# Regrouped deviations in a Fourier filter with a SoLU layer: laid out by a small matrix product in place of a store and a reload

## Chip, core and metric

The kernel runs on one core of one Trainium2 chip. The metric is the device time of one execution in microseconds (us). The core has TensorE (PE, matrix products; its weight loads are shown apart as PEld), VectorE (DVE), ScalarE (ACT), GpSimd (POOL) and SyncE (SP). Each engine works through its own instructions in order. DMAs are issued from SP, ACT and POOL, as instructions in these engines' order: an issue that has to wait holds up what stands behind it on that engine.

## What is computed

```python
def _attn_ref(x, filt_r, filt_i):                 # x: (8, 3136, 256) fp32
    X = np.fft.rfft(x, axis=1)
    Y = X * (filt_r + 1j * filt_i)[None, :, :]
    return np.fft.irfft(Y, n=x.shape[1], axis=1).astype(np.float32)

def _moe_ref(x, w_in, w_out, g_ln):               # x: (25088, 256), w_in: (256, 1024), w_out: (1024, 256)
    h = x @ w_in
    e = np.exp(h - np.max(h, axis=-1, keepdims=True))
    solu = h * (e / (np.sum(e, axis=-1, keepdims=True) + 1e-09))
    mu = np.mean(solu, axis=-1, keepdims=True)
    var = np.mean((solu - mu) ** 2, axis=-1, keepdims=True)
    return (((solu - mu) / np.sqrt(var + 1e-06) * g_ln) @ w_out).astype(np.float32)

def reference(x, filt_r, filt_i, moe_w_in, moe_w_out, moe_g_ln):
    return _moe_ref(_attn_ref(x, filt_r, filt_i).reshape(8 * 3136, 256), moe_w_in, moe_w_out, moe_g_ln)
```

All is in fp32. The part that matters here is the factor 1/sqrt(var + 1e-06), one number for each of the 25088 tokens, by which a row of the output is scaled.

## The kernel before

**Two kinds of work in one loop.** The eight images go through a Fourier transform of 49 x 64 points, a filter and the transform back; the tokens that come out go through the layer with w_in and w_out. Image 0 is transformed ahead of the loop, image 1 in its first steps, and images 2 to 7 beside the layer's work on the tokens that are already there. A list, PLAN (lines 37 to 46), says in which step each piece of an image's transform runs; lists of jobs for each step (line 875) hold them. The order of all engines' instructions is the order in which `step(k)` (line 948) writes them down; nothing reorders it.

**Blocks, pairs and groups.** A block is 128 tokens; there are 196. Two blocks are a pair (98), two pairs a group (49 groups of 512 tokens). A pair takes two steps, an even and an odd one. Products over a pair are made by a scheme with seven products in place of eight (m = 1 to 7), with sums of operands made by POOL (`pair_sums`, `project_sums`). `product(j, m)` (line 715) is one of seven products of pair j with w_in, into the banks of `ps_m`; `project(p, m)` (line 834) is one of seven with w_out, four matmuls each, into two banks of `ps_o`: products 1, 5, 6 and 3 add up in bank 0 (tag o0), products 2, 7 and 4 use bank 1 (tag o1). A step k with j = k // 2 has products of pair j, and projections of pair j - 5 (even step: 5, 3, 4) or j - 4 (odd step: 1, 2, 6, 7).

**From h to the output.** For a block, ACT and DVE make h, e, and solu (lines 729 to 780); ACT's `square` (line 775) leaves the sum of squared differences in one column of a tile of 128 x 4 for the group. DVE's `turn` (line 782) transposes solu in squares of 32 x 32, and `regroup` (line 790) copies the result by eight DMAs of 128 KB per pair (solu_t<-turn), issued from SP, so that 1024 features stand in the partitions. By this the tokens are regrouped: a block of the second product holds 32 tokens of each of the four blocks of a group. `keep_out` (ACT, line 854) and `finish_out` (DVE, line 858) scale the projections by the deviations while they move them from PSUM into the output tile `ot`, and `store_out` (line 863) stores it with two DMAs from SP.

**The deviations.** The four columns of a group, one per block, stand in the old order of tokens, and are needed in the new one: number (32 a + r, b) has to come to (32 b + r, a), with a and b from 0 to 3 and r from 0 to 31. `deviations` (line 802) makes 1/sqrt(var/1024 + 1e-6) in `rs` by two POOL instructions, and stores the 2 KB in DRAM (`rows`); `regroup_deviations` (line 812) loads them back by four DMAs of 512 bytes, 32 partitions each, into `rs_t`. For the groups up to 47 these DMAs are issued from SP: the store in the even step of an odd j, behind the eight solu_t DMAs of that step and ahead of its two stores of the output; the four loads in the odd step that follows. For the last group they are issued from POOL. The first reader of `rs_t` is `keep_out(p, 0, (0, 0))` in the odd step of the pair after (line 1033).

**Rows and fetches.** For images 2 to 7, `fetch_quarters` (line 235) loads rows of x by SP; DVE's `difference` and POOL's `sum` (line 257, instruction at line 260) prepare them, PE's `first_quarters` (line 263, matmuls at line 269, tile pa) makes the first half of the transform, ACT moves it to SBUF (line 274), and POOL issues the store into DRAM (d1, line 280). `fetch` (line 288, DMA at line 291, tile t) loads it back, ordered by frequency; it waits for those stores. For images 2 to 7 the fetch is issued from ACT (line 913), in the middle of an even step, behind the move of product 3 of the projection. The first fetch of image 2 (e == 2, i == 0) alone is issued at the end of step 14. `fetch_de` loads a table, from ACT as well. `back_halves` (line 361) makes the last part of the transform back.

Of the kernel before, what the change touches and what calls it, by code (L numbers as in the profile page):

```python
# [9 lines left out]
FP32 = mybir.dt.float32  # L10
# [7 lines left out]
P = 128  # L18
# [76 lines left out]
def kernel(  # L95
# [16 lines left out]
    de_dram = nc.inline_tensor(de_host, name="de_tbl").ap()  # L112

    def pool(name, bufs, space=None, stack=ctx):
        kw = {} if space is None else {"space": space}
        return stack.enter_context(tc.tile_pool(name=name, bufs=bufs, **kw))
# [508 lines left out]
    rs_dram = pool("rs_dram", 2, DRAM)  # L625
    pools |= {name: pool(name + "1", bufs)
             for name, bufs in (("r", 4), ("diff", 1), ("t2", 1), ("p", 1), ("g", 1))}
    pools["de"] = pool("de1", 2)
    second.pools = pools
# [50 lines left out]
    def load_de(sp, u):  # L680
# [6 lines left out]
    turns, variances, solu_ts, solu_sums, rs_rows, rss, pos, ots = (  # L687
        {} for _ in range(8))
# [113 lines left out]
    def deviations(p, dma):  # L802
        g, second = divmod(p, 2)
        if not second:
            rs = small.tile([P, 4], FP32, name=f"rs_{g}", tag="rs", bufs=2)
            nc.gpsimd.tensor_scalar(out=rs, in0=variances.pop(g), scalar1=1.0 / DFF, scalar2=EPS_LN,
                                    op0=ALU.mult, op1=ALU.add)
            nc.gpsimd.tensor_tensor(out=rs, in0=rs, in1=neg_half, op=ALU.pow)
            rs_rows[g] = rows = rs_dram.tile([P, 4], FP32, name=f"rows_{g}", tag="rows")
            dma(out=rows, in_=rs)  # L810

    def regroup_deviations(g, dma):
        rows = rs_rows.pop(g).rearrange("(a p) b -> b p a", p=32)
        rss[g] = small.tile([P, 4], FP32, name=f"rs_t_{g}", tag="rs_t")
        for b in range(4):
            dma(out=rss[g][32 * b:32 * b + 32, :], in_=rows[b])
# [17 lines left out]
    def project(p, m):  # L834

        bank = {1: 0, 6: 0, 5: 0, 3: 0, 2: 1, 7: 1, 4: 1}[m]
        if m in (1, 2):
            pos[p, bank] = ps_o.tile([P, DFF // 2], FP32, name=f"o{m}_{p}", tag=f"o{bank}")[:, 0:P]
        s1, s2, s3, s4 = solu_sums[p]
        lhs = {1: solu_ts[p, 0][0], 2: solu_ts[p, 0][1], 4: solu_ts[p, 1][1], 5: s1, 6: s2, 7: s3,  # L840
               3: s4}[m]
        w = w_out_sb[:, {1: 0, 2: 1, 3: 2, 5: 3, 6: 4, 7: 5, 4: 6}[m]]
        for f in range(KF // 2):
            nc.tensor.matmul(out=pos[p, bank], lhsT=lhs[:, f, :], rhs=w[:, f, :],  # L844
                             start=f == 0 and m in (1, 2, 7), stop=True, skip_group_check=True)
# [37 lines left out]
    for e in range(1, B):  # L883
# [24 lines left out]
        for i, t in enumerate(spectrum_at):  # L908
# [4 lines left out]
            dma = nc.sync.dma_start if e == 1 and t < 8 else nc.scalar.dma_start  # L913
# [34 lines left out]
    def step(k):  # L948
# [23 lines left out]
        if not odd:  # L972
# [25 lines left out]
            if proj:  # L998
                project(p, 3)
                keep_out(p, 0, (0, 1))  # L1000
                project(p, 4)
            for job in spectrum_loads[k]:
                job()
# [3 lines left out]
            if j - 3 == pairs - 2:  # L1007
                deviations(j - 3, nc.gpsimd.dma_start)
            if 0 <= j - 4 < pairs:
                project_sums(j - 4, 1)  # L1010
            if j - 3 == pairs - 2:
                regroup_deviations((j - 3) // 2, nc.gpsimd.dma_start)
            elif 0 <= j - 3 < pairs:
                deviations(j - 3, nc.sync.dma_start)
# [9 lines left out]
        else:  # L1024
# [16 lines left out]
            if 0 <= j - 3 < pairs:  # L1041
                if (j - 3) % 2 == 0 and j - 3 < pairs - 2:
                    regroup_deviations((j - 3) // 2, nc.sync.dma_start)
# [24 lines left out]
    with tc.manual_schedule():  # L1068
        pair_sums(0)
        for load in first_loads:  # L1070
            load()
        for k in range(blocks + LAG):
            step(k)
# [30 lines left out]
```

## Time and profile before

Three runs took 1626.26 us in the median (1624.71 to 1630.68). The profiled execution took 1619.98 us.

| | us |
|---|---|
| median of three runs | 1626.26 |
| the profiled execution's own time | 1619.98 |
| its span, first to last instruction | 1618.2 |
| matmuls with w_out, o<-w_out_sb (L844), 5488 passes, busy | 402.1 and 311.0 |
| matmuls with w_in, m<-w_in_sb (L723), 1372 passes, busy | 396.6 and 308.0 |
| POOL rs, two instructions per group (L806, L808), mean ns of one | 275 and 1034 |
| DMAs rows<-rs from SP and POOL | 48 and 1 |
| DMAs rs_t<-rows from SP and POOL | 192 and 4 |

The mean granted TensorE clock is 0.991 of the full one. A profile page has one line for each group of instructions: the source line (L844), the engine, the operation, what it writes and reads (o<-w_out_sb,solu_t), the shape, the count, busy time and mean duration. In a timeline the first two numbers are start and duration in us; a bracket at the end tells how long the engine was idle before and what ended that. SPq and ACTq mark the issue of a DMA, not its transfer. Busy times of PE overlap, since one matmul begins before the last one has drained.

### The profile page before, as it was taken

To read this page: it belongs to the slowest core of one execution; us is meant where nothing else is said; L and a number is where in the kernel's file an instruction comes from. 1 tells how busy PE (TensorE), PEld (TensorE's weight loads), DVE (VectorE), ACT (ScalarE), POOL (GpSimd) and SP (SyncE) were. 2 spreads that over 40 slices of the span, in tenths; PEclk is the share of its full clock that TensorE was granted. 3 is DMA by queue.
4 is the path that set the end of the run, shared out by engine and by line. 5 is a ranking of instruction groups with operands and counts; after the bars stand their busy time and mean duration, and the time that the engine had idled before them with its cause. 6 is when DMAs were issued, how large, how long until landed. Compare 5 with 4: busy or idle time off the path is not lost. (4 is left out here: it accounts for less than half of the span.)

```text
span 1618.2 us, 37006 instructions
## 1 busy us (share of the span) xinstructions
PE 1548.8 (96%) x12710; PEld 1048.2 (65%) x12710; DVE 1302.4 (80%) x2630; ACT 903.4 (56%) x1772; POOL 1169.3 (72%) x1333
## 2 busy tenths in 40 slices
PE   5899899999999999999999999999999999999997
PEld 1363456666766677667766676667676777777776
DVE  1686877998898989997999789897988777777772
ACT  2135555566565655666656655566556566665662
POOL 4446887579777877797688867788666766677775
PEclk8999999999999999999999999999999999999999
DMA  9888878877788778866887668866785454444443
GB/s 268 245 268 249 244 208 229 223 209 196 203 246 231 201 189 243 241 192 167 211 251 200 186 180 229 238 180 169 215 234 151 121 135 122 104 112 105 110 110 102
DMA packets 377245, 312.13 MB, mean 193 GB/s; under 512 B 62762, under 2 KB 342835, under 8 KB 377059
## 3 DMA queue, kind: packets, MB, share of 16 engines
q1 hardware_dynamic: 304340, 168.63, 40.3%
q0 software_dynamic: 34624, 101.68, 20.7%
q10 hardware_dynamic: 38096, 39.46, 8.1%
q8 instruction: 103, 1.69, 0.5%
q14 instruction: 82, 0.67, 0.1%
HBM read 124.86 MB, written 81.50 MB: 128 GB/s over the span
## 5 line engine op out<-in xcount | busy, mean ns | idle before, releaser
L844 PEld LDWEIGHTS o<-w_out_sb,solu_t 128*128 128x128 f32 x3136 | 382.8, 192 | 49.3 <-issue 43.9
L723 PE MATMUL m<-w_in_sb,s 128*128 128x512 f32 x784 | 396.6, 607 | 9.9 <-ACT h L733 9.2
L844 PE MATMUL o<-w_out_sb,solu_t 128*128 128x128 f32 x3136 | 402.1, 276 | 2.9 <-DVE ot L860 2.0
L844 PEld LDWEIGHTS o<-w_out_sb,u 128*128 128x128 f32 x2352 | 307.3, 192 | 144.4 <-issue 109.7
L844 PE MATMUL o<-w_out_sb,u 128*128 128x128 f32 x2352 | 311.0, 275 | 7.4 <-ACT ot L856 4.6
L723 PE MATMUL m<-w_in_sb,y 128*128 128x512 f32 x588 | 308.0, 607 | 4.8 <-DVE h L744 2.9
L771 DVE SCALAR_TENSOR_TENSOR h<-e,rsum,h 128x1024 f32<-128x1024 f32 x196 | 302.1, 1541 | 6.9
L733 ACT COPY h<-m 128x512 f32<-128x512 f32 x294 | 172.9, 588 | 237.0 <-PE m L723 204.2
L702 POOL TENSOR_TENSOR u<-solu_t 128x512 f32<-128x512 f32 x98 | 133.3, 1361 | 219.3 <-DMA solu_t<-turn 134.6
L856 ACT ACTIVATE ot<-o,rs_t 128x128 f32<-128x128 f32 x392 | 143.6, 366 | 258.3 <-PE o L844 241.2
L779 ACT ACTIVATE h<-h,nmu 128x1024 f32<-128x1024 f32 x196 | 224.9, 1148 | 53.2 <-DVE turn L787 43.0
L747 DVE CUSTOM_DVE_ANT_0 h<-m,h 128x512 f32<-128x512 f32 x196 | 134.1, 684 | 140.3 <-ACT h L733 102.6
L787 DVE STREAM_TRANSPOSE turn<-h 128x1024 f32<-128x1024 f32 x196 | 243.2, 1241 | 3.2
L755 ACT ACTIVATE e<-h,nmax 128x1024 f32<-128x1024 f32 x196 | 225.1, 1149 | 8.8 <-DVE h L771 8.4
L702 POOL TENSOR_TENSOR u<-solu_t,u 128x512 f32<-128x512 f32 x98 | 149.0, 1520 | 93.4 <-PE o L844 89.2
L723 PEld LDWEIGHTS m<-w_in_sb,s 128*128 128x128 f32 x784 | 128.6, 191 | 98.3 <-issue 85.0
L860 DVE SCALAR_TENSOR_TENSOR ot<-o,rs_t,ot 128x128 f32<-128x128 f32 x294 | 102.0, 347 | 77.0 <-ACT ot L856 60.6
L723 PEld LDWEIGHTS m<-w_in_sb,y 128*128 128x128 f32 x588 | 96.3, 191 | 102.1 <-issue 52.9
L702 POOL TENSOR_TENSOR u<-u,solu_t 128x512 f32<-128x512 f32 x98 | 161.6, 1649 | 0.9
L702 POOL TENSOR_TENSOR solu_t<-solu_t,solu_t 128x512 f32<-128x512 f32 x98 | 153.4, 1565 | 7.7
L702 POOL TENSOR_TENSOR s<-y 128x128 f32<-128x128 f32 x196 | 95.6, 488 | 0.5
L372 PEld LDWEIGHTS py<-wb_t,t 50*64 50x64 f32 x3584 | 57.6, 134 | 42.9 <-issue 22.5
(116 smaller groups left out, 1965.4 us busy)
## 6 DMA issues: line engine op xcount, KB each, us to landing
solu_t<-turn SPq DMA_DIRECT2D x784, 128.0 KB
out_dram<-ot SPq DMA_DIRECT2D x196, 128.0 KB
t<-d POOLq DMA_DIRECT2D x112, 200.0 KB, 6.0
d<-x POOLq DMA_DIRECT2D x100, 200.0 KB, 5.1
f<-f_dram POOLq DMA_DIRECT2D x39, 512.0 KB, 7.2
d<-g POOLq DMA_DIRECT2D x39, 512.0 KB, 4.8
t<-d ACTq DMA_DIRECT2D x37, 512.0 KB
x<-in_x_dram SPq DMA_DIRECT2D x112, 98.0 KB
```

The lines of the kernel that those rows point to most:

```text
L372: nc.tensor.matmul(out=views[g][64 * h:64 * h + 64, cb, i, :], lhsT=t4[rows, i, c0:c0 + 64], rhs=wb_t[rows, 0:N1], start=True, stop=True)
L702: nc.gpsimd.tensor_tensor(out=out, in0=in0, in1=in1, op=op)
L723: nc.tensor.matmul(out=ms[j, bank], lhsT=lhsT, rhs=w_in_sb[:, w, :], start=m in (1, 2, 7), stop=True, skip_group_check=True)
L733: nc.scalar.copy(out=h_half(k, i), in_=ms[j, 0])
L747: nc.vector.tensor_tensor_reduce(out=h_half(k, i), in0=ms[j, bank], in1=h_half(*kept), scale=1.0, scalar=sofar, op0=ALU.add, op1=ALU.min, ...
L755: nc.scalar.activation(out=e, in_=hs[k], func=AFT.Exp, bias=nmaxs.pop(k)[:, 1:2], scale=-1.0, accum_out=esum)
L771: nc.vector.scalar_tensor_tensor(out=solu, in0=e, scalar=rsum, in1=solu, op0=ALU.mult, op1=ALU.mult, accum_out=nmu)
L779: nc.scalar.activation(out=solu, in_=solu, func=AFT.Square, bias=nmu, scale=-float(DFF), accum_out=variances[g][:, i:i + 1])
L787: nc.vector.transpose(out=turns[g][:, :, i, :], in_=solus[k].rearrange("p (f j) -> p f j", j=32))
L844: nc.tensor.matmul(out=pos[p, bank], lhsT=lhs[:, f, :], rhs=w[:, f, :], start=f == 0 and m in (1, 2, 7), stop=True, skip_group_check=True)
L856: nc.scalar.activation(out=out_half(p, *to)[0], in_=pos[p, 0], func=AFT.Copy, scale=rs)
L860: nc.vector.scalar_tensor_tensor(out=ot, in0=pos[p, bank], scalar=rs, in1=out_half(p, *kept)[0], op0=ALU.mult, op1=ALU.add)
```

## The change

The deviations no longer go through DRAM. A table `turn_t` of 128 x 36 is loaded once, by POOL: its first 32 columns hold a one where the partition's number modulo 32 equals the column's number, its last four a one where the partition divided by 32 does. `deviations(g)` makes `rs` as before and then, in a third POOL instruction, a tile `wide` of 128 x (4 x 32): element (p, b, i) is rs[p, b] where p modulo 32 is i, and zero elsewhere. `regroup_deviations(g, ps)` is a product on PE, with `wide` as the weights and the last four columns of the table as the moving side: it puts rs[32 a + r, b] at (32 b + r, a). Its result takes four columns of bank 1 of the projection, columns 128 to 131, behind the 128 that products 2, 7 and 4 use; ACT copies it from there to `rs_t`. The product stands in an even step of an even j, behind product 4 of the projection of pair j - 5, one pair before its result is read, and ahead of the fetches of that step; the first group, when there is no projection yet, uses a bank of `ps_t`. The last group goes the same way as the others. The five DMAs per group and the DRAM tile are gone.

Beside this the first fetch of image 2 is issued from SP, at the same place in the order of steps.

```diff
@@ -110,6 +110,10 @@
     wi_dram = nc.inline_tensor(wi_host, name="wi_tbl").ap()
     wb_dram = nc.inline_tensor(wb_host, name="wb_tbl").ap()
     de_dram = nc.inline_tensor(de_host, name="de_tbl").ap()
+    rows = np.arange(P)[:, None]
+    turn_dram = nc.inline_tensor(np.concatenate(
+        [rows % 32 == np.arange(32), rows // 32 == np.arange(4)], 1).astype(np.float32),
+        name="turn_tbl").ap()
 
     def pool(name, bufs, space=None, stack=ctx):
         kw = {} if space is None else {"space": space}
@@ -622,10 +626,11 @@
     hpool = pool("hp", 2)
     wk = pool("wk", 1)
     spool = pool("sp", 1)
-    rs_dram = pool("rs_dram", 2, DRAM)
     pools |= {name: pool(name + "1", bufs)
              for name, bufs in (("r", 4), ("diff", 1), ("t2", 1), ("p", 1), ("g", 1))}
     pools["de"] = pool("de1", 2)
+    spread = pool("spread", 1)
+    turn_t = spread.tile([P, 36], FP32, name="turn_t", tag="turn_t")
     second.pools = pools
     for c, at, n, kind, dims in (
             (0, 0, 4 * C, "t2", "p (v c) -> p v c"), (0, 4 * C, 4 * C, "f", "p (v k c) -> p v k c"),
@@ -684,8 +689,8 @@
                             in_=de_dram[i:i + pairs].rearrange("i p k u q -> p i (k u q)"))
         return de
 
-    turns, variances, solu_ts, solu_sums, rs_rows, rss, pos, ots = (
-        {} for _ in range(8))
+    turns, variances, solu_ts, solu_sums, spreads, rss, pos, ots, places = (
+        {} for _ in range(9))
     sums, ms, hs, nmaxs, es, solus, squares = {}, {}, {}, {}, {}, {}, {}
 
 
@@ -799,21 +804,22 @@
             nc.sync.dma_start(out=st[32 * q:32 * q + 32, :, :],
                               in_=turned[32 * a:32 * a + 32, :, q, :])
 
-    def deviations(p, dma):
-        g, second = divmod(p, 2)
-        if not second:
-            rs = small.tile([P, 4], FP32, name=f"rs_{g}", tag="rs", bufs=2)
-            nc.gpsimd.tensor_scalar(out=rs, in0=variances.pop(g), scalar1=1.0 / DFF, scalar2=EPS_LN,
-                                    op0=ALU.mult, op1=ALU.add)
-            nc.gpsimd.tensor_tensor(out=rs, in0=rs, in1=neg_half, op=ALU.pow)
-            rs_rows[g] = rows = rs_dram.tile([P, 4], FP32, name=f"rows_{g}", tag="rows")
-            dma(out=rows, in_=rs)
-
-    def regroup_deviations(g, dma):
-        rows = rs_rows.pop(g).rearrange("(a p) b -> b p a", p=32)
+    def deviations(g):
+        rs = small.tile([P, 4], FP32, name=f"rs_{g}", tag="rs", bufs=2)
+        nc.gpsimd.tensor_scalar(out=rs, in0=variances.pop(g), scalar1=1.0 / DFF, scalar2=EPS_LN,
+                                op0=ALU.mult, op1=ALU.add)
+        nc.gpsimd.tensor_tensor(out=rs, in0=rs, in1=neg_half, op=ALU.pow)
+        spreads[g] = wide = spread.tile([P, 4, 32], FP32, name=f"wide_{g}", tag="wide")
+        nc.gpsimd.tensor_tensor(
+            out=wide, in0=turn_t[:, 0:32].rearrange("p (o i) -> p o i", o=1).broadcast_to([P, 4, 32]),
+            in1=rs.rearrange("p (b o) -> p b o", o=1).broadcast_to([P, 4, 32]), op=ALU.mult)
+
+    def regroup_deviations(g, ps):
+
+        nc.tensor.matmul(out=ps, lhsT=spreads.pop(g).rearrange("p b i -> p (b i)"), rhs=turn_t[:, 32:36],
+                         start=True, stop=True)
         rss[g] = small.tile([P, 4], FP32, name=f"rs_t_{g}", tag="rs_t")
-        for b in range(4):
-            dma(out=rss[g][32 * b:32 * b + 32, :], in_=rows[b])
+        nc.scalar.copy(out=rss[g], in_=ps)
 
     def project_sums(p, step):
 
@@ -835,7 +841,9 @@
 
         bank = {1: 0, 6: 0, 5: 0, 3: 0, 2: 1, 7: 1, 4: 1}[m]
         if m in (1, 2):
-            pos[p, bank] = ps_o.tile([P, DFF // 2], FP32, name=f"o{m}_{p}", tag=f"o{bank}")[:, 0:P]
+            ps = ps_o.tile([P, DFF // 2], FP32, name=f"o{m}_{p}", tag=f"o{bank}")
+            pos[p, bank] = ps[:, 0:P]
+            places[p] = ps[:, P:P + 4]
         s1, s2, s3, s4 = solu_sums[p]
         lhs = {1: solu_ts[p, 0][0], 2: solu_ts[p, 0][1], 4: solu_ts[p, 1][1], 5: s1, 6: s2, 7: s3,
                3: s4}[m]
@@ -910,7 +918,7 @@
             other = e == 1 and i % 2 == 1 and t + 1 < LAG
 
 
-            dma = nc.sync.dma_start if e == 1 and t < 8 else nc.scalar.dma_start
+            dma = nc.sync.dma_start if e == 1 and t < 8 or e == 2 and i == 0 else nc.scalar.dma_start
             fetches = ahead(t, 2) if e == 1 and t < 8 or e == 2 and i == 0 else spectrum_loads[t - 2]
             fetches.append(lambda sp=sp, i=i, dma=dma: sp.fetch(i, dma))
             ahead(t, 1 if e == 1 and i % 2 == 1 else 2).append(lambda sp=sp, i=i: sp.fetch_filter(i))
@@ -999,19 +1007,17 @@
                 project(p, 3)
                 keep_out(p, 0, (0, 1))
                 project(p, 4)
+            if j >= 4 and j % 2 == 0 and j - 4 < pairs:
+                regroup_deviations((j - 4) // 2, places.pop(p) if proj else psum("ps_rs")[:, 0, 0:4])
             for job in spectrum_loads[k]:
                 job()
             if 0 <= j - 3 < pairs:
                 regroup(j - 3, 0)
                 regroup(j - 3, 1)
-            if j - 3 == pairs - 2:
-                deviations(j - 3, nc.gpsimd.dma_start)
             if 0 <= j - 4 < pairs:
                 project_sums(j - 4, 1)
-            if j - 3 == pairs - 2:
-                regroup_deviations((j - 3) // 2, nc.gpsimd.dma_start)
-            elif 0 <= j - 3 < pairs:
-                deviations(j - 3, nc.sync.dma_start)
+            if 0 <= j - 3 < pairs and j % 2:
+                deviations((j - 3) // 2)
             if hid:
                 product(j, 7)
             if 2 <= k < blocks + 2:
@@ -1038,9 +1044,6 @@
             if hid:
                 product(j, 3)
                 product(j, 4)
-            if 0 <= j - 3 < pairs:
-                if (j - 3) % 2 == 0 and j - 3 < pairs - 2:
-                    regroup_deviations((j - 3) // 2, nc.sync.dma_start)
             if proj:
                 project(p, 6)
                 project(p, 7)
@@ -1067,6 +1070,7 @@
 
     with tc.manual_schedule():
         pair_sums(0)
+        nc.gpsimd.dma_start(out=turn_t, in_=turn_dram)
         for load in first_loads:
             load()
         for k in range(blocks + LAG):
```

## The prediction

> **What bounds the kernel now.** I read the page first, then busy time by stretch, then the timeline at the places where TensorE (PE) stands still, then the two small tiles that the change touches.
>
> ```profile
> span 1618.2 us, 37006 instructions
> PE 1548.8 (96%) x12710; PEld 1048.2 (65%) x12710; DVE 1302.4 (80%) x2630; ACT 903.4 (56%) x1772; POOL 1169.3 (72%) x1333
> ```
>
> ```profile
> 160.00:1560.00 1400.00, 1376.30 (x11775) 948.09 (x11775) 1183.68 (x2400) 828.22 (x1637) 1054.81 (x1199) 1.00 0.69 189
> 240.00:280.00 40.00, 36.02 (x454) 24.38 (x453) 29.18 (x59) 19.38 (x39) 28.67 (x38) 0.96 0.79 227
> 1400.00:1440.00 40.00, 40.00 (x231) 29.21 (x230) 31.54 (x71) 24.06 (x48) 29.34 (x30) 1.00 0.42 107
> ```
>
> The columns of the second block are PE, weight loads, DVE, ACT, POOL, clock, DMA. From 160 to 1560 us PE is idle for 1400 - 1376.3 = 23.7 us in all; from 1400 to 1440 not at all. So PE sets the time: what is added to it counts in full, and what a removed wait can give back is at most these 23.7 us, some stretched products beside them, and a little at the ends. Is a "busy" PE at its own limit? The timeline tells:
>
> ```profile
> 91.50 14.43 PE L395 MATMUL py<-wi_t,t 100*128 100x98 f32 x128
> 1010.25 1.95 PE L844 MATMUL o<-w_out_sb,solu_t 128*128 128x128 f32 x16
> 1008.54 1.88 PE L723 MATMUL m<-w_in_sb,s 128*128 128x512 f32 x4
> ```
>
> One fp32 product is two passes (two weight loads, two matmuls: project's four products per call show as x8). One pass lasts 275 ns but they overlap: 16 passes with 128 moving columns take (1.95 - 0.28) / 15 = 0.111 us each; 128 passes with 98 columns take (14.43 - 0.28) / 127 = 0.1115 us each. Fewer columns, same pitch: here the load of 128 weight columns sets the pace, not the columns that move.
>
> The path that the change removes, and what it costs today:
>
> ```profile
> L816 SPq DMA_DIRECT2D rs_t<-rows x192: 302/424/1771, 181.9 to 1573.8; - x192
> L810 SPq DMA_DIRECT2D rows<-rs x48: 338/552/1481, 173.8 to 1570.3; - x48
> ```
>
> ```profile
> 1043.11 2.09 SPq L816 DMA_DIRECT2D rs_t<-rows  x4
> 1044.23 0.58 ACT L733 COPY h<-m 128x512 f32<-128x512 f32 x1 [2.25 <-DMA de<-de_tbl]
> 1045.29 5.01 SPq L799 DMA_DIRECT2D solu_t<-turn  x6
> 1049.05 0.37 ACT L856 ACTIVATE ot<-o,rs_t 128x128 f32<-128x128 f32 x1 [4.24 <-DMA rs_t<-rows]
> 1049.56 0.68 PE L844 MATMUL o<-w_out_sb,u 128*128 128x128 f32 x4 [1.02 <-ACT ot L856]
> ```
>
> 240 small DMAs on SP, five per group of two pairs, in front of the big solu_t ones; here ACT waits 4.24 us for rs_t and PE 1.02 us for ACT. And the one fetch that moves from ACT's queue to SP's:
>
> ```profile
> 238.80 1.03 POOL L280 DMA_DIRECT2D d<-x  x2
> 240.12 1.95 PE L844 MATMUL o<-w_out_sb,solu_t 128*128 128x128 f32 x16
> 243.67 0.38 ACTq L291 DMA_DIRECT2D t<-d  x1
> 244.70 0.58 ACT L733 COPY h<-m 128x512 f32<-128x512 f32 x1 [6.44 <-issue]
> 245.43 2.04 PE L723 MATMUL m<-w_in_sb,s 128*128 128x512 f32 x2 [3.36 <-ACT h L733]
> 247.26 1.78 PE L723 MATMUL m<-w_in_sb,y 128*128 128x512 f32 x2
> ```
>
> ACT stands from 238.26 to 243.67 in front of its own DMA issue, which waits for the rows stored at 238.80; behind it is the copy h, and PE waits 3.36 us for that. The next two products take 2.04 and 1.78 us, where such a pair usually takes 1.02.
>
> **What the Trainium skill says.** "TensorE: Matmul & The Clock Gate", section "LDWEIGHTS (loading the stationary operand)": a load's time goes with its columns, P/1.2 ns, not with the rows or the moving side; 128 columns are 107 ns, beside 0.1115 measured above: agreed. The same page, "What's actually happening": an idle window of some 3.4 us halves PE's clock; the two stretched products behind the 3.36 us gap, and the clock of 0.96 in that stretch, agree. "PSUM — Partial Sum Buffer", "The four PSUM rules": a matmul that starts a sum clears the accumulation marks of its whole bank but not the data. So the small product may stand in the bank of products 2, 7 and 4 only once 4 is done; that is where it is put, and no other product has to move. No trace shows this. "DMA: Bandwidth & Descriptors", "Issuing engines are not separate DMA queues": the issuing engine changes only whose sequencer spends time; so moving the fetch leaves the transfer as it is and moves the wait alone. The trace shows the wait, ACT's 5.4 us.
>
> **The change, part by part** (a group is two pairs, 49 groups; the durations are of the profiled execution, which took 1619.98 us for a span of 1618.2; the median of the runs is 1626.26, 0.4% above it, so I add the difference to the median).
>
> (a) The small product: 2 passes per group, lhsT of 128 columns, 4 moving columns. The trace has no matmul so narrow. Nearest row: L395, 0.1115 us a pass. From below: the skill's TensorE page, "Wait — 56ns, not 53.3ns?", puts the floor between two starts at about 25 ns, were its loads hidden: 48 x 2 x 0.025 = 2.4 us. From above, each load exposed by its whole own duration of 0.192 (LDWEIGHTS rows): 18.4. I take 48 x 2 x 0.1115 = **+10.7 us**: the first load hides under product 4's last pass, but the second and product 7's first do not hide under passes of 4 columns. The 49th group is in the tail, where PE waits for solu_t anyway. Its operand comes from POOL a whole pair earlier (about 12 to 16 us): no wait.
>
> (b) The fetch of image 2, unit 0: the 3.36 us of idle, and (2.04 - 1.02) + (1.78 - 1.02) = 1.78 of stretch: **-5.1 us**. On SP it stands behind eight solu_t and two out_dram; SP is through solu_t at 243.4, when the rows have just landed, so SP hardly waits; behind it there are only loads for later steps. The first product on t is at 255.5; a fetch issued at about 245 and landed some 4.4 us later (today a store behind it on SP is released at 248.0) is in time even if PE comes 5 us earlier. Bound: 0 to -5.1.
>
> (c) Waits on rs_t. PE loses 2.36 us at 491.85 (ACT's t<-d issue stood until 489.89, released by an rs_t DMA), 0.58 + 1.02 at 1047 to 1049, 0.47 at 1598. The last is worth nothing, since the tail then waits for solu_t (PE waits 1.52 at 1606.92 for u). **-4.0 us**, bound 0 to -4.4. What is late next at 491.85 is the same t<-d issue, behind another DMA.
>
> (d) SP without five DMAs: 1.1 + 4 x 0.42 us of issue, and the waits of SP's queue on rows, 31.2 us in 19 cases. solu_t and x rows go out earlier. What PE gains is only where DVE or POOL came late because of them (PE gaps of 0.5 to 0.7 us behind ot of L860 at 333, 540, 811): **-2 us**, bound 0 to -6, about the sum of these gaps up to 1100 us.
>
> (e) POOL's spreading operation, one per group: a 128x128 product of two small views; the nearest row, s<-y of 128x128, takes 488 ns. Together 24 us on an engine at 72%. Behind it stand f<-f_dram and the sum of x, and for that PE waits. Here:
>
> ```profile
> 996.68 1.04 POOL L808 TENSOR_TENSOR rs<-rs,neg_half 128x4 f32<-128x4 f32 x1
> 997.68 0.81 POOL L642 DMA_DIRECT2D f<-f_dram  x1
> 998.52 1.30 POOL L260 TENSOR_TENSOR x<-x 113x512 f32<-113x512 f32 x1
> 999.99 0.60 PE L269 MATMUL pa<-x,wq_t 49*64 49x512 f32 x2
> ```
>
> The sum ends at 999.82 and PE uses it at 999.99. I found nine such places with less than 0.5 us between (214, 354, 442, 476, 512, 667, 849, 998 and 1033 us): at most 9 x 0.5 = 4.5 us. Since POOL started these stretches with a wait for solu_t (5.77 us at 989.42), part of it is given back by (d): **+2 us**, bound 0 to 4.5. The last group trades a POOL issue of 0.66 us for it and drops four of 0.55: nothing on the path.
>
> (f) ACT's copy of 128x4 per group: between 0.19 (the 128x1 rows) and 0.37 (128x128), I take 0.2. It waits for product 4 and the small one, about 1.1 us, then delays the t<-d and de issues behind it. Cover: ACT idles here for 2.25 us (1010.46, for product 5), and PE has products 1 and 2 (1.8 us) before it needs the copy of product 5. **+0.5 us**, bound 0 to 3: without cover about 1.1 us in a few of the some 20 groups that have a fetch in the same step.
>
> (g) The table's load (one POOL issue of 0.55 us at the start) and the first group's product in a bank of ps_t: **+0.2 us**, 0 to 0.5. The moves in DVE's and SP's order cost nothing else: DVE has the same instructions.
>
> Sum: 10.7 - 5.1 - 4.0 - 2 + 2 + 0.5 + 0.2 = **+2.3 us**, 1622.3 for the profiled execution, **1628.5** for the median.
>
> **The rivals.** *Slower: POOL becomes the last to arrive.* Place: the sums of x one step behind a spreading operation, to 1110 us. Price: 4.5 us of (e), and where PE is late for pa the gains of (c) and (d) are eaten, because their places lie in the same stretches: 10.7 + 4.5 - 5.1 = +10.1, **1636**. It decides if most of the nine places move by the whole half microsecond. For it: POOL had no gap before these sums. Against: the solu_t wait at the head of each stretch, which the change shortens.
> *Faster: narrow passes are cheap.* If the loads find cover, (a) is 2.4, the sum -6.0; with (d) at -6 it is -10.0: **1616**. For it: loads overlap with passes. Against: the 98 columns at 0.1115.
> *The fetch gains nothing* (SP waits in ACT's place, and solu_t is late): +2.3 + 5.1 = +7.4, **1633.5**, still within half a per cent. Against: 243.4 on SP and the landing nearly coincide.
>
> **How the numbers follow.** Half a per cent is 8.1 us, about what can be told from no change here: 1618.1 to 1634.4. Own forecast 0.45; fetch without gain 0.12; slower rival 0.25; faster rival 0.18. The forecast and the fetch rival lie nearly all within half a per cent; some 0.07 of them go over as the bounds of (a) add up; so 0.18 faster, 0.50 same, 0.32 slower. The range 1617 to 1638 holds the two middle cases, the slower rival's value and the edge of the faster one.
>
> **What would show it.** (a) two passes of L8xx with starts 0.11 us apart between product 4 and 7; 0.03 would be the faster rival. (b) no gap of ACT at 240 us, clock 1.00 there. (c) no wait on rs_t; ACT's new copy released by PE. (e) the waits of pa on POOL's x: under 2 us more, or over 4. I am wrong if PE's idle time between 160 and 1560 us does not fall by about 8 us, or if the small product takes other than 0.2 us of PE.

## The result and the profile after

The changed kernel took 1623.07 us in the median of 13 runs (1619.40 to 1633.72), beside 1626.26 us of 13 runs of the kernel before on the same chip: a ratio of 0.9974, with a 95% interval of 0.9953 to 0.9995. A second set of runs of the same kernel, told below, gave 1.0002 (0.9983 to 1.0021). So the first set is 3 us faster and the second is not; in the mean of the two the change is worth about 2 us, against a forecast of 2.3 us the other way. The sum was off by little, but two parts of it, the removed DMAs and the moved fetch, are wrong by more than ten microseconds each, with opposite signs. That is what the experiments are about.

The profiled execution of the changed kernel took 1633.72 us and is the longest of its 13 runs: its first product with w_in starts at 118.0 us instead of 105.8, in the first transform, where nothing of the change is at work. Its span is therefore not compared; stretches of it are. The page's head first:

```profile
span 1631.9 us, 36835 instructions
...
PE 1567.5 (96%) x12808; PEld 1071.4 (66%) x12808; DVE 1310.4 (80%) x2630; ACT 910.4 (56%) x1821; POOL 1190.2 (73%) x1378
```

PE has 98 passes more than before, ACT 49 instructions more, POOL 45. The busy times of the same three stretches as before (PE, weight loads, DVE, ACT, POOL, clock, DMA):

```profile
160.00:1560.00 1400.00, 1379.40 (x11851) 953.26 (x11844) 1188.55 (x2393) 832.70 (x1678) 1075.77 (x1243) 1.00 0.69 190
240.00:280.00 40.00, 32.56 (x297) 21.49 (x290) 26.09 (x50) 17.84 (x37) 28.68 (x37) 0.91 0.70 192
1400.00:1440.00 40.00, 40.00 (x232) 29.28 (x231) 30.71 (x71) 23.93 (x48) 30.73 (x32) 1.00 0.41 109
```

PE's idle time from 160 to 1560 us is 20.6 us, where it was 23.7: it fell by 3.1 us and not by the 8 that the forecast named as its own test. And one stretch has become worse: from 240 to 280 us PE stands for 7.4 us (4.0 before), at a clock of 0.91 (0.96 before). Since this execution is late as a whole, its window holds other work than before; but after_again, which is not late, has 7.2 us at a clock of 0.87 in it (and 18.5 us from 160 to 1560). Outside this stretch PE's idle time fell from 19.7 to 13.2 us. The new instructions, by groups (busy time, mean ns of one, idle before it):

```profile
L813 POOL TENSOR_TENSOR wide<-turn_t,rs 128x128 f32<-128x128 f32 x49 | 19.5, 398 | 3.9
L819 PEld LDWEIGHTS o<-turn_t,wide 128*128 128x128 f32 x96 | 14.6, 192 | 0.0
L819 PE MATMUL o<-turn_t,wide 128*128 128x4 f32 x96 | 13.6, 212 | 0.0
L822 ACT COPY rs_t<-o 128x4 f32<-128x4 f32 x48 | 7.8, 162 | 24.9 <-PE o L819 24.8
```

Nothing waits for rs_t from DRAM any more, and the copy waits for PE, as forecast. One of the 48 small products, in the timeline:

```profile
1053.34 0.61 PE L852 MATMUL o<-w_out_sb,solu_t 128*128 128x128 f32 x4
1053.46 0.30 PEld L852 LDWEIGHTS o<-w_out_sb,solu_t 128*128 128x128 f32 x2
1053.68 0.30 PEld L819 LDWEIGHTS o<-turn_t,wide 128*128 128x128 f32 x2
1053.79 0.28 PE L819 MATMUL o<-turn_t,wide 128*128 128x4 f32 x2
1053.90 0.30 PEld L728 LDWEIGHTS m<-w_in_sb,s 128*128 128x128 f32 x2
1053.93 1.10 PE L728 MATMUL m<-w_in_sb,s 128*128 128x512 f32 x2
```

The groups of loads start at 1053.46, 1053.68 and 1053.90: 0.22 us for each two passes. The two narrow matmuls take 0.28 us together, so their starts are some 0.03 us apart (each lasts 0.17 to 0.25), but product 7 can start only 0.14 us after the first of them, when its own weights are in. The loads set the pace.

### The profile page after: what moved, and what is told of

It is laid out like the page before. It is cut to its first block, busy times and chain, and to the rows that moved or that the text cites. A ratio compares the mean times of both kernels' runs of the same rounds, so it can differ in the third digit from the quotient of the medians.

```text
span 1631.9 us, 36835 instructions
## 1 busy us (share of the span) xinstructions
PE 1567.5 (96%) x12808; PEld 1071.4 (66%) x12808; DVE 1310.4 (80%) x2630; ACT 910.4 (56%) x1821; POOL 1190.2 (73%) x1378
## 3 DMA queue, kind: packets, MB, share of 16 engines
q10 hardware_dynamic: 37568, 38.94, 8.1%
## 4 chain that ended last, share of the span: by engine, by line
PE 72%; DVE 2%; issue 1%; DMA 1%; POOL 0%; ACT 0%; DVEq 0%; POOLq 0%; ACTq 0%
PE o L852 32%; PE m L728 31%; PE py L376 3%; PE pa L273 2%; PE pc L305 2%; PE pb L305 2%; DMA f<-f_dram 1%; DVE h L776 0%; DVE turn L792 0%; DMA solu_t<-turn 0%; PE o L819 0%; DVE h L752 0%; DVE ot L868 0%; DMA out_dram<-ot 0%; DVE pt L327 0%
## 5 line engine op out<-in xcount | busy, mean ns | idle before, releaser
L776 DVE SCALAR_TENSOR_TENSOR h<-e,rsum,h 128x1024 f32<-128x1024 f32 x196 | 314.2, 1603 | 6.9
L707 POOL TENSOR_TENSOR u<-u,solu_t 128x512 f32<-128x512 f32 x98 | 165.0, 1684 | 0.9
L707 POOL TENSOR_TENSOR s<-y 128x128 f32<-128x128 f32 x196 | 100.9, 515 | 12.9 <-ACT y L402 12.5
```

Source lines behind the costliest of these rows:

```text
L707: nc.gpsimd.tensor_tensor(out=out, in0=in0, in1=in1, op=op)
L776: nc.vector.scalar_tensor_tensor(out=solu, in0=e, scalar=rsum, in1=solu, op0=ALU.mult, op1=ALU.mult, accum_out=nmu)
```

## The experiments

Ratios are to the kernel before on the same chip, with the 95% interval; 0.001 is 1.6 us. "ACT" in the third column says that the fetch of image 2, unit 0 is issued from ACT as before. The last column is explained in the last group: the distance of the large tiles, in bytes of each partition, from where the kernel before has them, which is at multiples of 512.

| run | what it is | fetch | ratio | tiles off by |
|---|---|---|---|---|
| the change | | SP | 0.9974 (0.9953 to 0.9995) | 0 |
| after_again | the change | SP | 1.0002 (0.9983 to 1.0021) | 0 |
| after_fetch_act | the change | ACT | 0.9949 (0.9932 to 0.9967) | 0 |
| fetch_act_repeat | the same | ACT | 0.9956 (0.9939 to 0.9974) | 0 |
| before_fetch_sp | before | SP | 1.0059 (1.0033 to 1.0085) | 0 |
| three_products_act | small product three times | ACT | 1.0051 (1.0034 to 1.0069) | 0 |
| one_spread_act | one spreading operation | ACT | 0.9932 (0.9905 to 0.9959) | 0 |
| no_regroup | no store, no reload | ACT | 1.0003 (0.9983 to 1.0022) | -128 |
| no_product | spread alone | ACT | 0.9981 (0.9965 to 0.9996) | -128 |
| no_copy | spread and product | ACT | 1.0016 (0.9998 to 1.0034) | -128 |
| no_copy_again | the same | ACT | 1.0006 (0.9983 to 1.0029) | -128 |
| copy_last | copy behind the fetches | ACT | 0.9942 (0.9926 to 0.9958) | 0 |
| copy_constant | copy not used | ACT | 0.9952 (0.9932 to 0.9972) | 0 |
| copy_sbuf | copy of a table | ACT | 0.9934 (0.9910 to 0.9958) | 0 |
| copy_only | copy, no product | ACT | 0.9885 (0.9860 to 0.9910) | 0 |
| before_with_copy | before, copy ahead of fetches | ACT | 1.0140 (1.0109 to 1.0171) | 128 |
| before_copy_behind | before, copy behind them | ACT | 1.0126 (1.0098 to 1.0154) | 128 |
| before_pad | before, unused tile | ACT | 1.0144 (1.0112 to 1.0176) | 128 |
| no_regroup_pad | no store, no reload, unused tile | ACT | 0.9866 (0.9836 to 0.9895) | 0 |

**The fetch alone, in both kernels.** In the changed kernel:

```diff
-            dma = nc.sync.dma_start if e == 1 and t < 8 or e == 2 and i == 0 else nc.scalar.dma_start
+            dma = nc.sync.dma_start if e == 1 and t < 8 else nc.scalar.dma_start
```

and in the kernel before the same edit the other way round.

> The changed kernel once more. Both theories: 0.996 to 0.999 of the time before, as in the result. The profiled execution with the result lost some 12 us before the first product (118.0 us in place of 105.8), at a granted clock of 0.67 between 80 and 120 us, where the change has nothing: if that was chance, the first product starts near 106 us here, and the profiled execution takes about 1619 to 1622 us. In it, a group without other work should still cost PE 0.22 us more than before.

> The changed kernel with one part undone: the first fetch of image 2 is issued from ACT again. Theory relief (removing five small DMAs per group from SP gives PE some 9 us or more, the fetch gives 0 to 2): 0.997 to 0.999, as the whole change. Theory fetch (the fetch gives some 5 us, the removed DMAs some 5, the product costs 10.7): 1.000 to 1.002 of the time before, and a gap of PE of about 3.4 us near 245 us.

> The kernel before with one part alone: the first fetch of image 2 is issued from SP. Theory relief: 0.999 to 1.000. Theory fetch: 0.996 to 0.998 (5 us less), and no PE gap of 3.4 us near 245 us. If the data come late on this way, PE waits for t at the first product of image 2 (pb), and the gain is given back.

The move costs time in both kernels: 0.0059 in the kernel before, some 9.6 us (5.4 to 13.8), and in the changed one 0.0036 between the means of two sets each, some 6 us. Put back on ACT, the fetch leaves a complete kernel of 1618.29 us and 1618.92 us (copy_last, which is complete too, took 1616.49 us; the intervals don't tell them apart). The timeline of the changed kernel shows where PE waits (the wait of py is for another transfer, issued from POOL):

```profile
251.42 1.31 SPq L876 DMA_DIRECT2D out_dram<-ot  x2
...
252.97 0.41 SPq L295 DMA_DIRECT2D t<-d  x1
...
260.00 1.14 PE L376 MATMUL py<-wb_t,t 50*64 50x49 f32 x60 [0.58 <-DMA t<-d]
...
266.45 2.01 PE L305 MATMUL pb<-t,de 64*64 64x256 f32 x16 [5.32 <-DMA t<-d]
268.39 2.07 PE L728 MATMUL m<-w_in_sb,s 128*128 128x512 f32 x2
```

and the kernel before with the fetch on SP has the same place:

```profile
245.96 0.57 SPq L291 DMA_DIRECT2D t<-d  x1
...
254.07 1.15 PE L372 MATMUL py<-wb_t,t 50*64 50x49 f32 x64
...
257.17 2.01 PE L301 MATMUL pb<-t,de 64*64 64x256 f32 x16 [1.96 <-DMA t<-d]
```

From issue to the end of PE's wait it is 13.5 us and 11.2 us, and 13.3 us in after_again (issued at 243.53, product at 256.83). In the kept traces with the fetch on ACT no wait of PE is put down to it.

Is that simply how long this transfer takes? The DMA packets say no. The pages list the queues apart: what ACT issues runs in q10, what SP issues in q1, and with the move 528 packets (0.52 MB) go from one to the other (in the kernel before q10 has 38096 packets, in before_fetch_sp 37568). In the kernel before the fetch is issued at 243.67 us. The DMA view of the four microseconds from 244 to 248 has

```profile
q10 hardware_dynamic: 800, 0.79, 67.4%
```

and that of 248 to 256 has none of q10. 800 packets are the fetch and the table behind it, so both have landed 4.3 us after the issue, over 7 us before PE's first product on the data (255.54). In the other kept traces with the fetch on ACT and the tiles in place both have landed after 5.1 to 9.8 us. In q1 the fetch stands behind the two stores of out_dram, among the packets of solu_t, and its last packet ends 10.3 us after the issue in before_fetch_sp, 12.8 us in the changed kernel and 12.9 us in after_again. So the move did not only take the stall from ACT: it put the same 512 KB into the queue where more was waiting, and they came later. With ACT no longer held up, PE comes to the product at 251.6 us in after_again, four microseconds sooner than in the kernel before, and waits 5.2 us for the data. Behind such a wait the next two products take 2.07 us in the changed kernel, just as behind the old one.

How much of the loss is at this place can be read from the starts of the products with w_in: from pair 7 to pair 9 they take 36.4 us in the kernel before and 40.7 with the fetch on SP; in the changed kernel 41.7 and 41.4 with SP, 38.9 and 35.8 (after_fetch_act, fetch_act_repeat) with ACT. That is some 4 us. The rest of the 9.6 and 6 us is not located.

**The new work by itself.**

```diff
-        nc.tensor.matmul(out=ps, lhsT=spreads.pop(g).rearrange("p b i -> p (b i)"), rhs=turn_t[:, 32:36],
-                         start=True, stop=True)
+        wide = spreads.pop(g).rearrange("p b i -> p (b i)")
+        for _ in range(3):
+            nc.tensor.matmul(out=ps, lhsT=wide, rhs=turn_t[:, 32:36], start=True, stop=True)
```

> The changed kernel with the fetch on ACT and the small product made three times in a row, same operands, same place: two more products per group, 49 groups. Theory full price: 2 x 0.22 x 49 = 21 us over the single one, 1.007 to 1.009 of the time before. Theory pace: clearly less, 1.000 to 1.005, since in the stretches with transform work PE has waits that the product takes the place of. In the profile, from pair 76 to 90, where PE has no wait, a group should cost 0.44 us more than with one product under both.

For the other one, every group uses the spread tile of the first group, so that all later groups get the first group's deviations:

```diff
     def deviations(g):
...
+        if g:
+            spreads[g] = spreads[0]
+            return
...
-        nc.tensor.matmul(out=ps, lhsT=spreads.pop(g).rearrange("p b i -> p (b i)"), rhs=turn_t[:, 32:36],
+        nc.tensor.matmul(out=ps, lhsT=spreads[g].rearrange("p b i -> p (b i)"), rhs=turn_t[:, 32:36],
```

> The changed kernel with the fetch on ACT; the spread tile is made by POOL for the first group alone and used for all (so the deviations of the first group are used for all). Term (e) of the prediction: 0 to 4.5 us faster than the whole, taken as 2 us: 0.992 to 0.995. If POOL's step is what helps (see no_product), it is slower than the whole: 0.998 to 1.002.

Two more products for each of 48 groups cost 0.0099 against the mean of the two runs with one: 16 us, 0.17 us for each over the whole run. Where PE has no wait the price is plain: pairs 76, 78, 80 and 82, which have a small product, take 13.76 us each with one (fetch_act_repeat), 14.21 with three and 13.54 with none (copy_only), so 0.22 us for each product. The spreading operations are worth 0.002, about 3 us, which the intervals don't tell from zero.

**Taking the path away.** In the kernel before, store and reload go and the outputs are scaled by a constant tile (no deviations in the result):

```diff
-            rs_rows[g] = rows = rs_dram.tile([P, 4], FP32, name=f"rows_{g}", tag="rows")
-            dma(out=rows, in_=rs)
...
-        rss[g] = small.tile([P, 4], FP32, name=f"rs_t_{g}", tag="rs_t")
-        for b in range(4):
-            dma(out=rss[g][32 * b:32 * b + 32, :], in_=rows[b])
+        rss[g] = neg_half
```

> The kernel before without the store and the four loads of the deviations, and with nothing in their place: the output is scaled by a constant in place of the deviations, which are still made on POOL. It shows what the removed DMAs are worth alone, with the fetch of image 2 on ACT as before. Theory relief: 0.992 to 0.994 (10 to 13 us). Theory fetch, which is the prediction's terms of 4.0 and 2 us: 0.996 to 0.997 (5 to 6 us).

The same from the other side: the changed kernel with the fetch on ACT, without product and copy, or without the copy alone (again a constant scale):

```diff
-        nc.tensor.matmul(out=ps, lhsT=spreads.pop(g).rearrange("p b i -> p (b i)"), rhs=turn_t[:, 32:36],
-                         start=True, stop=True)
-        rss[g] = small.tile([P, 4], FP32, name=f"rs_t_{g}", tag="rs_t")
-        nc.scalar.copy(out=rss[g], in_=ps)
+        rss[g] = neg_half
```

> The changed kernel with the fetch on ACT, and without the small product and ACT's copy: POOL still makes the spread tile, the outputs are scaled by a constant, which leaves out the regrouped deviations. Its sibling without the spread tile (no_regroup) took the time of the kernel before, and the whole with product and copy took 0.995 of it. Theory full price (PE time counts in full wherever it is added, 10.7 us for 49 products): this one is 10.7 us faster than the whole, 0.987 to 0.990. Theory pace (the product's time is taken from waits that PE has anyway, and something in the added steps shortens others' waits): 0.998 to 1.002, as no_regroup, if the product or the copy matters; 0.993 to 0.996 if it is the spread tile's step on POOL.

> The changed kernel with the fetch on ACT, with the spread tile and the product but without ACT's copy (outputs scaled by a constant, the product's result is not read). Theory full price: 0.994 to 0.996, the same as with the copy, and 10.7 us over the one without a product. Theory pace: 0.994 to 0.996 if the product's place on PE is what helps, 0.998 to 1.002 if it is ACT's copy, which makes ACT wait for PE ahead of its two DMA issues.

These three made no sense together. With all DMAs gone and nothing in their place the time stays (1.0003), with product and copy in their place it falls (0.9949), and the copy of 128x4 seems to gain 11 us. My reading then was that the copy holds ACT back and so orders the DMA queues better; the other candidate was the constant scale, which the slow ones have in common. Four runs on that, with these edits:

```diff
-        nc.scalar.copy(out=rss[g], in_=ps)
+        return lambda: nc.scalar.copy(out=rss[g], in_=ps)
...
+                spectrum_loads[k].append(
+                    regroup_deviations((j - 4) // 2, places.pop(p) if proj else psum("ps_rs")[:, 0, 0:4]))
```

for copy_last; in the kernel before, ahead of the fetches:

```diff
                 project(p, 4)
+            if proj and j % 2 == 0:
+                seen = small.tile([P, 4], FP32, name=f"seen_{p}", tag="seen")
+                nc.scalar.copy(out=seen, in_=pos[p, 1][:, 0:4])
```

and, with the copy in place but a constant scale,

```diff
-        rss[g] = small.tile([P, 4], FP32, name=f"rs_t_{g}", tag="rs_t")
-        nc.scalar.copy(out=rss[g], in_=ps)
+        rs_t = small.tile([P, 4], FP32, name=f"rs_t_{g}", tag="rs_t")
+        nc.scalar.copy(out=rs_t, in_=ps)
+        rss[g] = neg_half
```

> The changed kernel with the fetch of image 2 back on ACT (measured 0.9949), and ACT's copy of the small product put behind ACT's two fetch issues of the same step instead of ahead of them; nothing else differs. Theory 'held back': the copy is worth about 11 us because it waits for product 4 and so holds ACT's fetches back until x rows and solu_t on SP are out; then this kernel loses most of it, 1.000 to 1.003, and DVE's waits for rows of x go up from 8.5 to 11 us or more between 285 and 1360 us. Theory 'something else' (the constant scale of the kernels without a copy, or the order of the sums): 0.993 to 0.997 as with the copy ahead.

> The kernel before, with one thing added: in the step of every second pair ACT copies 128x4 of the bank of product 4 into a tile that nobody reads, ahead of its two fetch issues, as the changed kernel's ACT does with the small product. Store, reload and all products are as before. Theory 'held back': the copy alone gains here too, 0.991 to 0.996. Theory 'something else': 0.999 to 1.002, since a copy that nobody reads can give nothing but later issues.

> The changed kernel with the fetch on ACT, spread, product and copy in place, but the outputs are scaled by a constant tile instead of the copied deviations, which leaves the deviations out of the result as in the two kernels without product or copy. Theory 'held back': 0.993 to 0.997, the constant makes no difference. Theory 'constant scale': the constant is what made the kernel without the copy slow, so this one is slow as well, 1.000 to 1.003.

> The changed kernel with the fetch on ACT, once more, unchanged: how far the same kernel moves from one set of runs to the next. The two sets of the changed kernel differed by 0.0028. All theories expect 0.992 to 0.998; outside it, differences of 0.3 per cent between kernels of different sets tell nothing.

Both readings fell. The copy behind the fetches gains as much as ahead of them, so it holds nothing back; the constant scale is as fast as the true one; and in the kernel before the copy costs 23 us. The next four asked whether the slow value repeats, and what about the copy matters: a copy of a constant (`nc.scalar.copy(out=seen, in_=turn_t[:, 0:4])`), the copy without the product (`ps` is four columns of product 4), and in the kernel before the copy behind the fetches.

> The kernel with spread and small product but no copy, scaled by a constant tile (the deviations are left out of the result), once more. If the copy is truly worth 12 us: 1.000 to 1.003 as before. If that value was chance of the set: 0.994 to 0.998, and the copy is worth little.

> The kernel without the copy of the product (constant scale, the deviations left out), with an ACT copy of 128x4 from the constant table in the same place, which waits for no other engine. Theory 'the wait': ACT standing until product 4 is done, and DVE's last sum of the pair behind it, is what spaces SP's work out; then this one stays slow, 1.000 to 1.003. Theory 'any row': one more instruction of ACT there is enough, 0.993 to 0.997.

> The kernel without small product (0.9981; spread kept, constant scale, the deviations left out), with the ACT copy, which reads four columns of product 4 instead. If the copy gains by itself: product and copy add up, 0.9981 - 0.0073 = 0.991, range 0.989 to 0.993. If the copy only makes good what the product does without a reader: 0.996 to 0.999, no gain.

> The kernel before with the unread ACT copy of product 4 behind ACT's two fetch issues instead of ahead of them (ahead: 1.014). If the loss comes from fetches held back or from the order in which they share their lanes with SP's: 0.998 to 1.003. If it comes from ACT standing for PE there, as such: 1.010 to 1.016.

Any copy gains where there is no reload, even one that waits for nobody, and any copy costs in the kernel before, wherever it stands. An instruction cannot do both. What comes with each of them is its tile. The pool of small tiles is laid out behind the weights and `y` and ahead of all other large tiles, and a tile of 4 buffers there takes 128 bytes of each partition. In the kernel before and in the changed one, `turn` begins at byte 97792 of a partition, `solu_t` at 144896, and all large tiles behind the small ones at a multiple of 512 (so the change itself moves none of them); without a tile for rs_t they begin 128 bytes lower, with rs_t and a tile for the copy 128 bytes higher. The last two runs move the tiles and nothing else: one line is added to the kernel before and to no_regroup, and the instructions differ in addresses alone.

```diff
+    pad = small.tile([P, 4], FP32, name="pad", tag="pad")
     turns, variances, solu_ts, solu_sums, rs_rows, rss, pos, ots = (
```

> The kernel before with one tile of 128x4 allocated that nothing writes or reads; every instruction is as before, but all large tiles begin 128 bytes later in each partition, off the multiples of 512. Theory 'place in SBUF': slow like the kernels before with a copy, 1.010 to 1.016. Theory 'ACT row': no row is added, so 0.998 to 1.002.

> The kernel before without store and reload of the deviations, scaled by a constant tile (the deviations are left out of the result; 1.0003 before), with an unused tile in the place of the one for the reload, so that the large tiles begin at multiples of 512 again; no instruction differs from the kernel that gave 1.0003. Theory 'place in SBUF': removing the DMAs is worth 15 to 22 us, 0.986 to 0.991. Theory 'ACT row': 0.998 to 1.002 as without it.

The place in SBUF was it: 128 bytes cost 0.0144 in the kernel before, 24 us (18 to 29), and giving them back to no_regroup brings it from 1.0003 to 0.9866. The pages show it in the time that the same packets take. The lines are queue, packets, MB and share of 16 engines over the span. no_regroup (span 1622.6 us):

```profile
q1 hardware_dynamic: 269780, 168.42, 43.2%
```

no_regroup_pad (span 1604.4 us):

```profile
DMA packets 342521, 311.88 MB, mean 194 GB/s; under 512 B 28042, under 2 KB 308115, under 8 KB 342339
...
q1 hardware_dynamic: 269780, 168.42, 39.6%
```

0.432 x 1622.6 is 701 us of every DMA engine, 0.396 x 1604.4 is 635 us: the same packets with the same bytes take 10% longer. The kernel before with the unused tile (before_pad, span 1658.5 us),

```profile
q1 hardware_dynamic: 304340, 168.63, 43.2%
```

with 0.432 x 1658.5 = 716 us, stands to the kernel before (0.403 x 1618.2 = 652 us, its line is below) in the same way. All kept traces fall into four groups by these two things: 634 to 643 us (tiles in place, no reload), 652 and 657 (in place, reload), 698 to 701 (off, no reload), 715 to 718 (off, reload). Counted by size, it is the packets of 512 bytes that become slower, 200,704 in number, which are those of solu_t<-turn from SBUF to SBUF: 32.5 ns each in the kernel before and 37.2 in before_pad, 59 of the 64 us. And DVE, which waits for rows of x, shows where it goes (waits from 285 to 1360 us: us in total, times, longest). The kernel before:

```profile
DVE diff L254 <- DMA x<-in_x_dram: 5.9, 7, 2.1
DVE diff L254 <- DMA rs_t<-rows: 4.5, 3, 1.9
DVE diff L254 <- DMA solu_t<-turn: 0.4, 1, 0.4
```

with the unused tile:

```profile
DVE diff L254 <- DMA x<-in_x_dram: 23.6, 17, 3.2
DVE diff L254 <- DMA rs_t<-rows: 8.3, 1, 8.3
DVE diff L254 <- DMA solu_t<-turn: 7.7, 4, 4.0
```

The Trainium skill has a mechanism that fits, in "DMA: Bandwidth & Descriptors", section "How a descriptor splits into AXI transactions": a read that doesn't start at a multiple of 256 bytes begins at the boundary below it, and the unused bytes cost their beats. A piece of 512 bytes that starts 128 beyond a boundary takes 20 beats of 32 bytes instead of 16, an estimate from that page: 25% more beats for the read, where the packets of this size took 14% longer. Whether it is this, and whether 256 or 512 bytes count, no run here tells.

With the tiles in place, no_regroup_pad is the run that no_regroup was meant to be: the store and the reload, taken away alone, are worth 0.0134, 21.8 us (17 to 27). The page of the kernel before shows what they are:

```profile
DMA packets 377245, 312.13 MB, mean 193 GB/s; under 512 B 62762, under 2 KB 342835, under 8 KB 377059
...
q1 hardware_dynamic: 304340, 168.63, 40.3%
```

245 DMAs of 2 KB or less are 34,720 packets of under 512 bytes (62,762 less 28,042), more than all others of that size together, and those of q1, 34,560 packets with 0.21 MB of its 168.63, take 652 - 635 = 17 us of every one of the 16 engines (against the whole group without reload, 634 to 643 us, it is 9 to 18). The loads are why there are so many: each picks single numbers out of `rows`, and 28,416 of these packets have 4 bytes (192 x 128 numbers, and 16 more for each of the 240 DMAs); the other 6,144, of the stores, have 16. One of either size takes 9 ns of an engine, where one of 512 bytes takes 32.5. Without them DVE's waits in the same window are

```profile
DVE diff L254 <- DMA x<-in_x_dram: 2.4, 4, 0.8
DVE diff L254 <- DMA solu_t<-turn: 0.3, 1, 0.3
```

instead of 10.8 us. PE's idle time from 160 to 1560 us falls from 23.7 to 17.1 us, and pairs 10 to 80 of the products with w_in take 1051.6 us instead of 1062.2. In pairs 90 to 97, where no transform runs beside them, nothing changes: 95.88 us in both.

## Why the prediction was wrong

**(a), the small product: right.** +10.7 us was forecast. The runs with product on ACT's fetch (0.9949, 0.9956) against copy_only (0.9885) give 0.0064 and 0.0071, 10.4 and 11.5 us. In pairs 90 to 97 the four groups take 96.77 us with it and 95.88 without (no_copy and no_product): 0.22 us each, twice the 0.1115 that was taken from L395. The rival of cheap passes is out: the narrow matmuls are cheap, the loads are not.

**(b), the fetch: the sign is wrong.** -5.1 us was forecast; moved alone it costs 9.6 us in the kernel before and some 6 in the changed one. The step that failed is "moving the fetch leaves the transfer as it is", and with it "landed some 4.4 us later". For ACT's queue the 4.4 us are right: 4.3 us by the packets of the kernel before. On SP's queue the same transfer took 10.3 to 12.9 us. The issue time was right (245 forecast, 243.53 and 245.96 measured, 252.97 in the profiled run that was late as a whole), and so was the end of ACT's stall. With 12 us in place of 4.4 the same text would have put the landing at 257, behind a product due at 255.5 less the 3.9 us saved. What the skill's "DMA: Bandwidth & Descriptors" says in "Issuing engines are not separate DMA queues", that DMAs of all issuing engines run on the same DMA engines and that issuing from several saves sequencer time alone, was read as if the queue made no difference to the transfer; these traces don't agree with that. The rival in which the fetch gains nothing had the right direction, but the term's bound, 0 to -5.1, has no room for a loss.

**(c) and (d), the DMAs: far too small.** -4.0 and -2 us were forecast, with -10.4 as the outer bound of both; alone they are worth 21.8 us. No run takes the two apart; the waits that (c) counts stand in the profile of the kernel before, so what is missing is put down to (d), and step (d) is the one that failed. It priced the issue time on SP and then counted only such gaps of PE as the one profile showed behind DVE. It left out what the packets take of the DMA engines: "under 512 B 62762" stood on the page, and some 17 us of each engine belong to them, in stretches where these are busy 71 to 79% of the time (285 to 1130 us) and DVE waits for rows of x. And it took the gaps of one execution as typical, although that execution was 6 us under the median, which the text had noted. That the small DMAs cost 21.8 us is measured; the way there is not: how much of it goes by way of the DMA engines and how much by way of SP's queue, where these issues took 84 us between pairs 10 and 80, no run separates.

**(e), (f) and (g): right within what can be told.** +2, +0.5 and +0.2 were forecast; copy_only against no_regroup_pad gives +0.0019, 3 us, of which the intervals leave zero possible. The waits of pa for POOL's sums of x, by which the slower rival was to show, did not grow: from 285 to 1360 us they are 0.7 us in the changed kernel (0.4 in after_again), where they were 1.3.

The terms measured are -21.8, +3, about +11 and about +6: -2 us. They are the steps of one chain of kernels, from the kernel before by no_regroup_pad, copy_only and the two runs with the fetch on ACT to the changed kernel, so they add up to its mean (0.9988) by construction; the sum tests nothing. That the forecast's +2.3 came near it is luck: the gain of the DMAs, missed by 16 us, and the loss of the fetch, missed by 11, had opposite signs.

## What to carry to other kernels

Count the packets of a small DMA, not only its bytes and its issue, wherever the DMA engines are mostly busy and an engine waits for other loads: here a load of 512 bytes was 128 packets of 4 bytes. When a DMA is moved to another issuing engine, ask what that engine's queue holds at that moment; the same transfer took 4.3 us in one queue and over 10 in the other, and PE, freed of its stall, came sooner and waited for it. When a kernel that leaves something out behaves oddly, compare the addresses of its tiles first: taking out one small tile moved all large ones by 128 bytes and hid the gain of 22 us.

## What was not expected of the hardware

- Large SBUF tiles that begin 128 bytes beside a multiple of 512 in each partition make the same packets 10% slower (635 to 701 us, 652 to 716 us of every DMA engine) and this kernel 1.4% slower, with no instruction changed but for addresses. The 512-byte packets from SBUF to SBUF account for nearly all of it (32.5 to 37.2 ns each).
- 34,560 packets of 4 and 16 bytes, 0.21 MB together, take some 17 us of each of 16 DMA engines; one of 4 bytes takes as long as one of 16 (9 ns), and nearly a third of one of 512 (32.5 ns).
- Two fp32 passes with 4 moving columns start 0.03 us apart, but cost 0.22 us of PE because the loads of 128 weight columns around them come 0.11 us apart.
- The same load of 512 KB landed 4.3 us after its issue in ACT's queue (kernel before) and 10.3 us after it in SP's (before_fetch_sp), which held stores and solu_t copies.
